# Linear-attention block on one Trainium2 core: trailing steps behind the third sum's copy, half of the last norm on VectorE, kv times wo in float32r parts

## The chip, the core and the metric

The kernel runs on one core of one Trainium2 chip. The core has a matrix engine (TensorE, PE), three engines for elementwise work (VectorE or DVE, ScalarE or ACT, GpSimd or POOL) and a queue engine (SyncE, SP) that here only starts DMA transfers; ACT and POOL start some too. Each engine works through its own instructions strictly in the order in which the program issued them, and waits at the head of that order until what it needs is there. The metric is the device time in microseconds (us) from start to end of one execution.

## The reference, cut to what matters

```python
def _A_ref(x, wqkv, wo):            # linear attention, 32 heads of 16
    qkv = (x @ wqkv).reshape(B, S, 3, H, Dh).transpose(2, 0, 3, 1, 4)
    q, k, v = qkv
    phi = lambda t: where(t > 0, t + 1, exp(t)) + 1e-6
    pq, pk = phi(q), phi(k)
    kv = einsum("bhsd,bhse->bhde", pk, v)
    z = einsum("bhsd->bhd", pk)
    num = einsum("bhqd,bhde->bhqe", pq, kv)
    den = einsum("bhqd,bhd->bhq", pq, z)[..., None] + 1e-6
    return (num / den).transpose(0, 2, 1, 3).reshape(B, S, D) @ wo

def _B_ref(x, w1, b1, w2):          # Dense -> Mish -> Dense
    h = x @ w1 + b1
    return (h * tanh(softplus(h))) @ w2

mod = (silu(c) @ w_mod).reshape(c.shape[0], 6, 1, -1)
sa, ca, ga, sb, cb, gb = six rows of mod
h = layernorm(x) * (1 + ca) + sa
x = x + ga * _A_ref(h, wqkv, wo)
h = layernorm(x) * (1 + cb) + sb
x = x + gb * _B_ref(h, w1, b1, w2)
```

The shapes are S = 2048 rows, D = 512 columns, F = 1792 hidden columns, all float32.

## The kernel before

**Precision.** Nearly every matrix product is made of three float32r products. split() makes of a tile t a high part (ACT copies t into float32r) and, one step later, a low part (DVE takes t minus the high part). mm3() adds hi x hi, hi x lo and lo x hi in PSUM. Only a few products take plain float32, among them m_ps at line 849: kv times wo, one matmul for each of four column groups, shown by the profile as eight instructions.

**Rows and tiles.** The 2048 rows are four blocks b of 512; a block is four tiles t of 128 rows. The working memory is one pool of 101 slots of 128x512 float32 (SLOTS); a tile takes a slot when it is made and gives it back after its last reader. PSUM has eight banks: four "acc", three "h", one "tp"; tiles of a tag take its banks in turn.

**The order of the work.** It is written out by hand. Work on DVE, ACT and POOL that follows a product is put into generators. spawn() adds one to a list and tick() moves every one in the list on by a step, the earliest spawned first. So the order on each engine is the order of the ticks, and within a tick the order of spawning. later(p, f, wait) waits `wait` steps and then issues the Mish of p on ACT; mish() issues Mish and high part in one step and the low part in the next.

**Attention.** wo_scale (line 474) multiplies the four tiles of wo by a row of the modulation, one tile a step, while PE builds gacc and q. z_side and kv_side prepare the small matrices that give den and kv. kv_ps (lines 830 to 840) is multiplied by a mask into kv; m_ps (847 to 850) is kv times wo, and its split parts ms are used by every o_unit. attend(b) (line 682) makes the reciprocal of den (lines 691 and 692), stores it in DRAM, loads it back spread over partitions as rd, scales q with it (706) and splits it into qs. o_unit(b, t) multiplies qs by ms; o_post adds the result to the rows r.

**The second norm.** Blocks 0 and 1 are normed before the pair stage. The eight tiles of blocks 2 and 3 are normed within it by norm_tile (line 764): first two ACT passes with sums (act_sums, lines 213 and 214), a step later a small DVE operation (218) and POOL's power (192), a step later DVE's shift nb (222) and the apply on ACT (201), a step later a POOL DMA of the tile to DRAM (775). They are read back at the start of the last pair (load_back).

**The pair stage.** The hidden layer works on pairs of row blocks and pairs of hidden tiles: a pair g makes four results c11, c12, c21, c22 of seven products (product, line 924), each two chunks of three matmuls. pair_begin makes a11 x b11 into bank pa, copies it (L940, u1), and adds a12 x b21 (c11). pair_early makes s1 x t1 into bank pc and adds s2 x t2 onto pa, copied as u2 (L958; L999 for the second of two pairs). pair_middle adds s3 x t3 onto pa, copied as u3 (L965), and c22 = pc + u3 (DVE, L935). pair_end adds a22 x t4 onto pa, whose Mish is taken straight from the bank (L899), and s4 x b22 onto pc, for c12. Since products add onto pa after a copy has read it, each copy must be done before PE writes the next.

pair_unit takes two functions as `between`: one ahead of pair_middle and one behind it. In the stage for blocks 0 and 1 (main stage) they are trail(): a norm tile is spawned, d_unit(0, f) multiplies an earlier activation by w2 (12 matmuls), and a tick follows. two_pairs interleaves pairs 0 and 1; its between[0] is a plain tick. In the stage for blocks 2 and 3 they are gap(): an e_unit and a tick. w2_job scales and splits a tile of w2 for each of two hidden tiles a pair, rows(g, wait) makes the left operands of pair g.

Of the kernel before, what the change touches and what calls it, by code (L numbers as in the profile page):

```python
# [13 lines left out]
P = 128  # L14
# [11 lines left out]
def block_kernel(ctx: ExitStack, tc: tile.TileContext, x, wqkv, wo, w1, b1t, w2, c, wmodt, out):  # L26
# [15 lines left out]
    def ps(tag, name, shape=(P, 512)):  # L42
        return psp.tile(list(shape), F32, tag=tag, name=name, bufs=PBUFS[tag])
# [4 lines left out]
    running, fresh = [], []  # L48

    def spawn(gen):  # L50
        fresh.append(gen)

    def tick():

        running.extend(fresh)
        fresh.clear()
        for g in list(running):
            if next(g, "end") == "end":
                running.remove(g)
# [11 lines left out]
    def split(name, t, keep, key, lo_engine=dve, hi_engine=act, plus=None):  # L71

        hi, lo = sb(f"{name}h", F32R, t.shape), sb(f"{name}l", F32R, t.shape)
        if hi_engine is act:
            act.activation(hi, t, AF.Copy)
        else:
            hi_engine.tensor_copy(hi, t)
        if lo_engine is dve:
            yield
        if plus is None:  # L80
            lo_engine.tensor_tensor(lo, t, f32(hi), op=ALU.subtract)
        else:
            dve.scalar_tensor_tensor(lo, t, plus, f32(hi), op0=ALU.add, op1=ALU.subtract)
        keep[key] = hi, lo
# [101 lines left out]
    def ln_eps(key, b, lo=0, hi=4):  # L186
        dve.tensor_scalar(rs[key, b][:, lo:hi], mv[key, b][:, lo:hi, 1], EPS, 1.0, op0=ALU.add, op1=ALU.mult)  # L187
# [11 lines left out]
    def ln_apply(key, b, j, t, dst, engine):  # L199
        if engine is act:  # L200
            act.activation(dst, t, AF.Identity, bias=nb[key, b][:, j:j + 1], scale=rs[key, b][:, j:j + 1])  # L201
        else:
            engine.tensor_scalar(dst, t, mv[key, b][:, j, 0:1], rs[key, b][:, j:j + 1],
                                 op0=ALU.subtract, op1=ALU.mult)

    def act_sums(key, b, t, v):

        if (key, b) not in rs:
            for d, name in (rs, "rs"), (nb, "nb"):
                d[key, b] = cst.tile([P, 4], F32, tag=name, name=f"{name}_{key}_{b}", bufs=NB)  # L210
        scrap = sb(f"scrap_{key}_{b}_{t}")
        sums = cst.tile([P, 2], F32, tag="sums", name=f"sums_{key}_{b}_{t}", bufs=6)
        act.activation(scrap, v, AF.Identity, scale=-1.0 / D, accum_out=sums[:, 0:1])
        act.activation(scrap, v, AF.Square, bias=sums[:, 0:1], accum_out=sums[:, 1:2])
        return sums

    def sums_eps(key, b, t, sums):
        dve.tensor_scalar(rs[key, b][:, t:t + 1], sums[:, 1:2], 1.0 / D, EPS, op0=ALU.mult, op1=ALU.add)  # L218
        ln_rstd(key, b, t, t + 1)

    def sums_shift(key, b, t, sums):
        dve.tensor_tensor(nb[key, b][:, t:t + 1], sums[:, 0:1], rs[key, b][:, t:t + 1], op=ALU.mult)
# [251 lines left out]
    def wo_scale():  # L474

        for k in range(4):
            dve.tensor_tensor(wos[k], wos[k], bc["ga"], op=ALU.mult)
            yield

    zc = cst.tile([P, 4], F32, name="zc")  # L480
    zh = cst.tile([P, 32], F32, name="zh")
# [282 lines left out]
    def norm_tile(b, t):  # L764

        v = xt.pop(("r", b, t))
        sums = act_sums("n", b, t, v)
        yield
        sums_eps("n", b, t, sums)
        yield  # L770
        sums_shift("n", b, t, sums)
        ln_apply("n", b, t, v, v, act)
        yield
        d = nd[b, t] = drp.tile([P, D], F32, name=f"nd_{b}_{t}")
        pool.dma_start(d, v)
# [51 lines left out]
    next(early_rows[1])  # L827
    attending = attend(0, 5)
    next(attending)
    kv_ps = ps("acc", "kv_ps")  # L830
    for g in range(4):
        for k in range(4):
# [3 lines left out]
    for j in range(2):  # L836
        js = slice(64 * j, 64 * (j + 1))
        dve.tensor_tensor(kv.rearrange("p (g m) -> p g m", g=4)[js, :, js],
                          kv_ps.rearrange("p (g m) -> p g m", g=4)[js, :, js],
                          bmask[js, js].unsqueeze(1).to_broadcast([64, 4, 64]), op=ALU.mult)  # L840
    next(attending)
    spawn(attending)
    for g in range(1, 4):
# [2 lines left out]
        tick()  # L846
    for g in range(4):
        m_ps = ps("acc", f"m_ps_{g}")
        pe.matmul(m_ps, kv[:, P * g:P * (g + 1)], wos[g], start=True, stop=True)
        spawn(split(f"m_{g}", m_ps, ms, g))  # L850
    run(early_rows[1])
    for g in range(4):
# [92 lines left out]
    def later(p, f, wait=0):  # L945
        for _ in range(wait):
            yield
        mish_b(p, f)
        yield
# [12 lines left out]
    def pair_middle(g, pa, pc, u2):  # L962
        u3, c22 = sb(f"u3_{g}"), sb(f"c22_{g}")
        product(g, "s3", "t3", onto=pa)
        act.activation(u3, pa, AF.Copy)  # L965
        add(c22, pc, u3)
        spawn(later(c22, 2 * g + 1))

    def pair_end(c0, g, pa, pc, u2):
        c12 = sb(f"c12_{g}")  # L970
        m = mish(product(g, "a22", "t4", onto=pa), c0, 2 * g + 1)
        next(m)
        spawn(m)
        product(g, "s4", "b22", onto=pc)
        add(c12, pc, u2)
        spawn(later(c12, 2 * g, 1))
        tick()

    def pair_unit(c0, g, odd, between):
        begun = pair_begin(c0, g, ("tp" if odd else "h", "h"))  # L980
        tick()
        state = pair_early(c0, g, *begun, "h")
        tick()
        between[0]()
        pair_middle(g, *state)
        between[1]()
        pair_end(c0, g, *state)

    def two_pairs(c0, g0, g1, begun, between):

        s0 = pair_early(c0, g0, *begun[0], "h")
        tick()
        pc = product(g1, "s1", "t1", "h")
        pair_middle(g0, *s0)
        tick()
        pa, c11 = begun[1]
        u2 = sb(f"u2_{g1}")
        product(g1, "s2", "t2", onto=pa)
        act.activation(u2, pa, AF.Copy)  # L999
        spawn(mish(c11, c0, 2 * g1))  # L1000
        tick()
        pair_end(c0, g0, *s0)
        between[0]()
        pair_middle(g1, pa, pc, u2)
        between[1]()
        pair_end(c0, g1, pa, pc, u2)

    def prep_a(b, f):
# [4 lines left out]
    def second(b, side):  # L1013

        for n, f in enumerate(last_first):
            side(n)
            ahead(b, n + NF)
            tick()
            d_unit(b, f, n)
# [34 lines left out]
    def norm_next():  # L1054
        if tiles:
            spawn(tiles.pop(0))

    def trail(f, side=None):
        def unit():
            norm_next()  # L1060
            d_unit(0, f, f)
            ahead(1, f)
            if side is not None:
                spawn(side)
            tick()
        return unit

    for g in range(1, G):
        for f in (2 * g, 2 * g + 1):
            spawn(w2_job(f))  # L1070
        if g == 1:
            spawn(rows(2, 3))
            norm_next()
            two_pairs(0, 0, 1, begun, (tick, trail(0, rows(3, 2))))
            store_rows(0)
        else:
            norm_next()
            pair_unit(0, g, g % 2, (trail(2 * g - 3), trail(2 * g - 2, rows(g + 2, 2) if g + 2 < G else None)))
        if g < KEPT:
            store_rows(g)  # L1080
        if g == G - 1:
            for n in range(8):
                load_back("n", nd, 2 + n // 4, n % 4)
    for f in (NF - 3, NF - 2, NF - 1):
        trail(f)()
    second(1, prepare)


# [28 lines left out]
    def e_unit(c, n):  # L1117
        g = pairs[n]
        seventh(("m1", "m2")[c], "acc", ag[L, 2 * g + c], [w[:, c, :] for w in wb[g]], n, G - 1)
# [66 lines left out]
    for n, g in enumerate(pairs):  # L1186
        if n < 5:
            if n:
                load_rows(n)
            if n:  # L1190
                load_wb(pairs[n + 1])
        if n == 5:
            load_wb(pairs[6])
            load_r(0, 0)
        if n == 6:
            for m in pairs[:5]:
                load_wt("m4", m)
        def gap(c, m):
            def unit():
                if m >= 0:  # L1200
                    e_unit(c, m)
                tick()
            return unit

        if n == 0:
            begun = [pair_begin(L, pairs[i], ("tp" if i else "h", "acc")) for i in range(2)]
            tick()
        elif n == 1:
            two_pairs(L, pairs[0], g, begun, (gap(0, 0), gap(1, 0)))
            for i in range(2):  # L1210
                spawn(left_trail(pairs[i]))
        else:
            pair_unit(L, g, n % 2, (gap(0, n - 1), gap(1, n - 1)))
            if n < EARLY:
                spawn(left_trail(g))
# [70 lines left out]
```

## Time and profile before

| what | value |
|---|---|
| median of 3 runs | 506.92 us (506.33 to 507.45) |
| the profiled execution | 505.36 us, span 503.6 us |
| mean granted TensorE clock | 0.997 |
| PE busy, matmuls | 492.7 us (98%), 2648 |
| DVE busy | 343.8 us (68%) |
| ACT busy | 294.4 us (58%) |
| POOL busy | 144.8 us (29%) |
| DMA | 98.58 MB, mean 196 GB/s |

The span is the time from the first to the last instruction; the execution's own time has some 1.8 us around it. Busy time of PE is not PE at its peak, since matmuls are pipelined and a record lasts longer than the distance to the next. A wait is written as the idle time before an instruction and what ended it. The shares are averages over stages of very different kind, so stretches of the span have to be read by themselves.

### The profile page before, as it was taken

The numbers are of one execution on the slowest core, as the hardware profiler recorded it, in microseconds if no ns is written. First come the engines' busy times: TensorE is split into PE (matmuls) and PEld (weight loads), VectorE is DVE, ScalarE is ACT, GpSimd is POOL, SyncE is SP. The second block draws the span as 40 slices with busy tenths as digits, with TensorE's granted clock in tenths as the row PEclk, the third lists the DMA queues.
The fourth block names the chain that finished last, engine by engine and source line by source line (L and its number), as shares of the span: only waits on it lengthen the run. The fifth ranks groups of instructions, "written<-read, shape, count | busy, mean of one in ns | idle before, by whom it ended". The sixth has DMA issues, their size and how long they took to land.

```text
span 503.6 us, 7666 instructions
## 1 busy us (share of the span) xinstructions
PE 492.7 (98%) x2648; PEld 414.0 (82%) x2648; DVE 343.8 (68%) x666; ACT 294.4 (58%) x532; POOL 144.8 (29%) x246
## 2 busy tenths in 40 slices
PE   7999999999999999998999999999999999999997
PEld 6788888878778888886778888888788888899997
DVE  6885664878987678966557562679953755559772
ACT  6868684724462978567988555368354555568100
POOL 3473120000213323123144210524355131445200
PEclk9999999999999999998999999999999999999999
DMA  8824753482554317439989935999999353698512
GB/s 289 297 68 88 194 128 87 129 270 72 140 136 131 84 42 235 147 117 376 303 282 336 361 123 192 285 373 337 366 366 283 90 158 83 147 230 229 127 43 85
DMA packets 66765, 98.58 MB, mean 196 GB/s; under 512 B 7405, under 2 KB 31861, under 8 KB 66726
## 3 DMA queue, kind: packets, MB, share of 16 engines
q0 software_dynamic: 29360, 45.31, 32.6%
q1 hardware_dynamic: 37220, 52.51, 32.0%
q8 instruction: 21, 0.34, 0.3%
q10 hardware_dynamic: 146, 0.26, 0.1%
q14 instruction: 18, 0.15, 0.1%
HBM read 62.92 MB, written 33.03 MB: 191 GB/s over the span
## 4 chain that ended last, share of the span: by engine, by line
PE 87%; ACT 6%; DVE 2%; issue 2%; DMA 1%; SPq 0%; DVEq 0%; ACTq 0%
PE p_a L930 16%; PE p_s L930 6%; PE m L69 5%; PE m L68 5%; PE m L67 5%; PE oacc L69 4%; PE oacc L68 4%; PE oacc L67 4%; PE o L67 3%; PE pq L67 3%; PE gacc L68 3%; PE gacc L69 3%; PE o L69 3%; PE gacc L67 3%; PE pq L69 3%; PE pq L68 3%
## 5 line engine op out<-in xcount | busy, mean ns | idle before, releaser
L935 DVE TENSOR_TENSOR c<-p_s,u 128x512 f32<-128x512 f32 x28 | 19.4, 692 | 47.1 <-PE p_s L930 25.4
L922 ACT ACTIVATE ub<-c,b1c 128x512 f32<-128x512 f32 x28 | 20.1, 718 | 7.5 <-DVE c L935 7.5
L958 ACT ACTIVATE u<-p_a 128x512 f32<-128x512 f32 x12 | 7.1, 593 | 29.4 <-PE p_a L930 29.4
L192 POOL TENSOR_TENSOR rs_n<-rs_n,half 128x1 f32<-128x1 f32 x16 | 11.1, 698 | 39.4 <-DVE rs_n L218 29.0
L1184 POOL DMA_DIRECT2D wt_m<-w2t x20 | 14.0, 704 | 26.1 <-PE m L69 17.2
L248 DVE SCALAR_TENSOR_TENSOR ku<-e_k,relu_k 128x512 f32<-128x512 f32 x16 | 11.0, 690 | 14.5 <-ACT relu_k L246 14.5
L788 ACT ACTIVATE hf_n<-tp_n,mc 128x512 f32<-128x512 f32 x16 | 11.7, 769 | 13.4 <-PE tp_n L786 13.4
L245 ACT ACTIVATE e_q<-pq 128x512 f32<-128x512 f32 x16 | 9.4, 588 | 16.3 <-PE pq L69 16.3
L940 ACT ACTIVATE u<-p_a 128x512 f32<-128x512 f32 x14 | 8.3, 596 | 17.8 <-PE p_a L930 17.8
L245 ACT ACTIVATE e_k<-pk 128x512 f32<-128x512 f32 x16 | 9.6, 598 | 13.3 <-PE pk L69 13.2
L586 POOL DMA_DIRECT2D w2b<-w2d x20 | 10.6, 549 | 18.1 <-DMA out_dram<-r 5.5
L899 ACT ACTIVATE u<-p_a,b1c 128x512 f32<-128x512 f32 x14 | 9.6, 683 | 9.9 <-PE p_a L930 9.9
L694 POOL DMA_DIRECT2D rden_d<-rden x3 | 2.2, 718 | 43.5 <-DVE rden L692 43.5
L935 DVE TENSOR_TENSOR c<-p_a,u 128x512 f32<-128x512 f32 x14 | 9.6, 690 | 7.2 <-PE p_a L930 2.4
L580 POOL DMA_DIRECT2D wb<-w2d x14 | 9.9, 712 | 14.8 <-PE m L69 8.2
L248 DVE SCALAR_TENSOR_TENSOR q<-e_q,relu_q 128x512 f32<-128x512 f32 x16 | 11.0, 688 | 4.5 <-ACT relu_q L246 4.3
L706 DVE SCALAR_TENSOR_TENSOR q<-q,rd 128x512 f32<-128x512 f32 x16 | 10.6, 688 | 4.7 <-DMA rd<-rden_d 4.7
L192 POOL TENSOR_TENSOR rs_x<-rs_x,half 128x1 f32<-128x1 f32 (+1 forms) x10 | 7.4, 744 | 22.2 <-DVE rs_x L187 21.4
L201 ACT ACTIVATE x<-x,nb_x,rs_x 128x512 f32<-128x512 f32 x15 | 11.5, 810 | 3.8 <-DVE nb_x L196 3.1
L718 DVE TENSOR_TENSOR r<-o,r 128x512 f32<-128x512 f32 x16 | 10.9, 679 | 2.3 <-PE o L69 2.3
L257 POOL DMA_DIRECT2D ku<-ku x8 | 7.2, 895 | 17.6 <-DVE ku L248 16.9
L965 ACT ACTIVATE u<-p_a 128x512 f32<-128x512 f32 x14 | 8.3, 591 | 6.2 <-PE p_a L930 6.2
(1427 smaller groups left out, 1944.1 us busy)
## 6 DMA issues: line engine op xcount, KB each, us to landing
wm<-in_wmodt_dram SPq DMA_DIRECT2D x24, 256.0 KB, 5.4
w2b<-w2d POOLq DMA_DIRECT2D x20, 256.0 KB, 6.6
wt_m<-w2t POOLq DMA_DIRECT2D x20, 256.0 KB, 3.4
r<-in_x_dram SPq DMA_DIRECT2D x16, 256.0 KB, 3.0
x<-in_x_dram SPq DMA_DIRECT2D x15, 256.0 KB, 4.8
w1p<-in_w_dram SPq DMA_DIRECT2D x14, 256.0 KB, 4.2
w2r<-in_w_dram SPq DMA_DIRECT2D x14, 256.0 KB, 3.2
wb<-w2d POOLq DMA_DIRECT2D x14, 256.0 KB, 4.3
```

The lines of the kernel that those rows point to most:

```text
L67: pe.matmul(o, st[0], mv[0], start=start, stop=False)
L68: pe.matmul(o, st[0], mv[1], start=False, stop=False)
L69: pe.matmul(o, st[1], mv[0], start=False, stop=stop)
L192: pool.tensor_tensor(y, y, half[:, lo:hi], op=ALU.pow)
L201: act.activation(dst, t, AF.Identity, bias=nb[key, b][:, j:j + 1], scale=rs[key, b][:, j:j + 1])
L245: act.activation(e, p, AF.Exp)
L248: dve.scalar_tensor_tensor(dst, e, 1.0, r, op0=ALU.min, op1=ALU.add)
L788: act.activation(hf[b, j], p, AF.Identity, bias=mc[:, 12 + j:13 + j], scale=mc[:, 16 + j:17 + j])
L922: act.activation(u, p, AF.Mish, bias=b1c[:, f:f + 1])
L930: pe.matmul(p, st, mv, start=onto is None and c == 0 and i == 0, stop=c == 1 and i == 2, skip_group_check=onto is not None)
L935: dve.tensor_tensor(out, p, u, op=ALU.add)
L1184: pool.dma_start(v, w2t[g][:, :, SUM[name], :])
```

## The change

There are three parts.

- **Ticks within a pair.** trail() and gap() no longer tick. pair_unit and two_pairs tick themselves: once behind pair_middle and once behind between[1]. So the trailing steps that came after the first d_unit or e_unit, ahead of the third sum, are now issued behind its copy u3 and c22. later(c22) gets one more step of waiting. In two_pairs between[0] of the main stage stays a tick ahead of pair_middle.
- **The last norm.** trail() spawns a norm tile only where it is given a `side`, so a pair takes two tiles in place of three. Tiles with odd t take DVE's statistics (bn_stats, bn_aggr), POOL's power in the same step, and DVE's apply a step later; tiles with even t stay as they were.
- **kv times wo.** wo_scale also splits each scaled tile, kv is split after its mask, and m_ps takes mm3 on the parts.

```diff
     def spawn(gen):
-        fresh.append(gen)
+        fresh.append(iter(gen))
...
         for k in range(4):
             dve.tensor_tensor(wos[k], wos[k], bc["ga"], op=ALU.mult)
             yield
+            yield from split(f"wos_{k}", wos[k], wos, k)
...
         v = xt.pop(("r", b, t))
-        sums = act_sums("n", b, t, v)
-        yield
-        sums_eps("n", b, t, sums)
-        yield
-        sums_shift("n", b, t, sums)
-        ln_apply("n", b, t, v, v, act)
+        if t % 2:
+            ln_stats("n", b, t, v)
+            ln_eps("n", b, t, t + 1)
+            ln_rstd("n", b, t, t + 1)
+            yield
+            ln_apply("n", b, t, v, v, dve)
+        else:
+            sums = act_sums("n", b, t, v)
+            yield
+            sums_eps("n", b, t, sums)
+            yield
+            sums_shift("n", b, t, sums)
+            ln_apply("n", b, t, v, v, act)
         yield
...
+    kvs = {}
     kv_ps = ps("acc", "kv_ps")
...
+    spawn(split("kv", kv, kvs, 0))
     next(attending)
...
-        pe.matmul(m_ps, kv[:, P * g:P * (g + 1)], wos[g], start=True, stop=True)
+        mm3(m_ps, [h[:, P * g:P * (g + 1)] for h in kvs[0]], wos[g], True, True)
...
         add(c22, pc, u3)
-        spawn(later(c22, 2 * g + 1))
+        spawn(later(c22, 2 * g + 1, 1))
...
         between[0]()
         pair_middle(g, *state)
+        tick()
         between[1]()
+        tick()
         pair_end(c0, g, *state)
...
         between[0]()
         pair_middle(g1, pa, pc, u2)
+        tick()
         between[1]()
+        tick()
         pair_end(c0, g1, pa, pc, u2)
...
     def trail(f, side=None):
         def unit():
-            norm_next()
+            if side is not None:
+                norm_next()
+                spawn(side)
             d_unit(0, f, f)
             ahead(1, f)
-            if side is not None:
-                spawn(side)
-            tick()
         return unit
...
-            pair_unit(0, g, g % 2, (trail(2 * g - 3), trail(2 * g - 2, rows(g + 2, 2) if g + 2 < G else None)))
+            pair_unit(0, g, g % 2, (trail(2 * g - 3), trail(2 * g - 2, rows(g + 2, 2) if g + 2 < G else ())))
...
     for f in (NF - 3, NF - 2, NF - 1):
         trail(f)()
+        tick()
...
         def gap(c, m):
             def unit():
-                if m >= 0:
-                    e_unit(c, m)
-                tick()
+                e_unit(c, m)
             return unit
```

## The prediction

> **What bounds the kernel now.** The page puts TensorE (PE) at 492.7 us busy of a 503.6 us span, so I looked for where PE does not run at its own pace. The first view was the busy time by stretch, cut at the starts of the column-pair products; its columns are the length, busy us (count) of PE, weight loads, VectorE (DVE), ScalarE (ACT) and GpSimd (POOL), then granted clock, DMA share and GB/s.
> ```profile
> 214.36:234.82 20.46, 18.36 (x74) 14.49 (x73) 11.58 (x23) 15.53 (x30) 5.75 (x10) 0.92 0.65 222
> 234.82:250.90 16.08, 15.29 (x67) 12.31 (x66) 9.58 (x22) 12.66 (x26) 3.24 (x5) 1.00 0.95 327
> 250.90:267.59 16.69, 15.42 (x68) 12.47 (x67) 9.83 (x23) 14.95 (x33) 6.85 (x12) 1.00 0.93 305
> 282.55:297.51 14.96, 14.96 (x68) 12.39 (x67) 9.34 (x17) 8.49 (x16) 3.20 (x6) 1.00 0.63 211
> 362.72:447.00 84.28, 84.28 (x441) 72.56 (x441) 44.36 (x71) 42.53 (x69) 33.17 (x55) 1.00 0.73 199
> ```
> A pair has seven products of 6 matmuls and two d_units of 12, 66 matmuls. Pair 5 does them in 14.96 us, 0.227 each, without a gap: that is PE's own pace. Pair 2 takes 16.08 (1.12 lost) and pair 3 16.69 (1.73 lost). The two interleaved pairs 0 and 1 have 72 matmuls from 214.36, 16.33 us at that pace, and take 20.46: 4.13 lost. The later pair stage (362.72 on) loses nothing, so reordering can only cost there. The most that the moved steps can bring is 6.98 us. The order of PE's instructions over time names the waits (start, duration, engine, line, in brackets the idle time and its releaser):
> ```profile
> 230.36 0.50 PE L930 MATMUL p_a<-t_0h,a_1h 128*128 128x512 f32 x1 [2.10 <-ACT u L965]
> 230.70 0.40 PE L930 MATMUL p_a<-t_0l,a_1h 128*128 128x512 f32 x1
> 231.18 0.63 PE L930 MATMUL p_a<-t_1h,a_1h 128*128 128x512 f32 x1
> 231.61 0.63 PE L930 MATMUL p_a<-t_1l,a_1h 128*128 128x512 f32 x1
> 234.59 0.39 PE L930 MATMUL p_s<-b_3h,s_1l 128*128 128x512 f32 x1
> ...
> 248.05 0.50 PE L930 MATMUL p_a<-t_0h,a_2h 128*128 128x512 f32 x1 [0.80 <-ACT u L965]
> ...
> 264.57 0.50 PE L930 MATMUL p_a<-t_0h,a_3h 128*128 128x512 f32 x1 [1.27 <-ACT u L965]
> ```
> All three wait for L965, the copy u3 of the third sum. The first has a second price: from 231.18 to 234.59 matmuls start 0.43 apart instead of 0.23 (231.18 to 231.61; granted clock 0.92 over the stretch), about 1.8 of the 4.13.
>
> **Why u3 is late, and what the moved steps do.** ACT's order in the two pairs, and DVE's row that holds it up:
> ```profile
> 221.86 0.73 ACT L922 ACTIVATE ub<-c,b1c 128x512 f32<-128x512 f32 x1 [0.76 <-DVE c L935]
> 223.80 0.82 ACT L201 ACTIVATE r<-r,nb_n,rs_n 128x512 f32<-128x512 f32 x1 [0.72 <-DVE nb_n L222]
> 224.52 0.71 ACT L899 ACTIVATE u<-c,b1c 128x512 f32<-128x512 f32 x1
> ...
> 229.12 0.70 ACT L922 ACTIVATE ub<-c,b1c 128x512 f32<-128x512 f32 x1
> 229.73 0.57 ACT L965 ACTIVATE u<-p_a 128x512 f32<-128x512 f32 x1
> 223.61 0.15 DVE L222 TENSOR_TENSOR nb_n<-sums_n,rs_n 128x1 f32<-128x1 f32 x1
> ```
> From 223.80 ACT runs back to back to u3 of pair 1 at 229.73.
>
> *Two pairs: slower by 0.62.* In this unit the step ahead of the third sum of pair 1 (between[0], here a plain tick) stays where it was; only the later gap moves. What changes is later(c22) of pair 0: with one more yield its Mish (ub, 221.86) no longer fills the time in which ACT waits for nb, but comes behind the apply of 223.80 (norm_tile was spawned earlier and steps first). The apply still starts at 223.80, since DVE's order up to nb is unchanged, so 0.62 (229.12 to 229.73) is inserted into the full chain: u3 near 230.35, PE's a22 near 230.98 instead of 230.36. From below the bound is 0 (the step finds a hole), from above 0.62 plus a longer slow-clock stretch, at most another 1.8. I take +0.62: the chain has no hole. The stall of 2.1 becomes 2.7 and the slow clock stays.
>
> *Pairs 2 and 3: faster by 2.85.* Here the tick with the trailing steps goes behind u3 and c22, and the three norm tiles of a pair become two, one on each engine. An ACT tile costs two passes and an apply, and an odd tile's price on DVE is in the rows of norm_each and of a scaled copy:
> ```profile
> 239.96 0.62 ACT L213 ACTIVATE scrap_n<-r 128x512 f32<-128x512 f32 x1
> 240.70 0.72 ACT L214 ACTIVATE scrap_n<-r,sums_n 128x512 f32<-128x512 f32 x1
> 241.42 0.58 ACT L958 ACTIVATE u<-p_a 128x512 f32<-128x512 f32 x1
> ...
> 182.47 0.70 DVE L183 BATCH_NORM_STATS2 st_n<-r 128x6 f32<-128x512 f32 x1
> 183.21 0.18 DVE L184 BATCH_NORM_AGGREGATE mv_n<-st_n 128x2 f32<-128x6 f32 x1
> L500 DVE TENSOR_SCALAR zs<-zbc_sb,mc 128x512 f32<-128x512 f32 x4 | 1.7, 480 | 0.0
> ```
> Passes 1.46 (239.96 to 241.42) and apply 0.72 (223.80 to 224.52): 2.18 a tile on ACT, 6.5 a pair before, 2.2 after; ACT falls from 14.95 in pair 3 to near 10.6 of 14.96. DVE gains 0.70 + 0.18 + 0.15 + 0.48 = 1.5 a pair (apply between 0.48 and the 0.69 of a two-input pass) on about 9.6. The added pow of an odd tile is queued on POOL behind the even tile's store, and DVE's apply waits for it one tick later; its result is wanted only by a store. Neither engine is full. Pair 4 shows when u3 can run once ACT is free, and DVE's trailing steps:
> ```profile
> 275.43 1.28 DVE L526 TENSOR_TENSOR w2r<-w2r,gb_bc 128x512 f32<-128x512 f32 x2
> 276.64 0.68 DVE L81 TENSOR_TENSOR a_8l<-u,a_8h 128x512 fp32r<-128x512 f32 x1
> 277.78 0.69 DVE L935 TENSOR_TENSOR c<-p_s,u 128x512 f32<-128x512 f32 x1 [0.46 <-ACT u L965]
> 278.39 0.68 DVE L81 TENSOR_TENSOR s_5l<-s,s_5h 128x512 fp32r<-128x512 f32 x1
> 277.15 0.60 ACT L965 ACTIVATE u<-p_a 128x512 f32<-128x512 f32 x1 [0.34 <-PE p_a L930]
> ```
> The pair starts at 267.59, so u3 is at +9.56 and c22 at +10.19. PE wants u3 at +12.24 (54 matmuls): 2.1 us of slack. I take the whole loss of both pairs away; the bounds are 0 and 2.85.
>
> *What is late next: +0.5.* Everything behind c22 on DVE now starts at +10.8: two low parts (0.60 each, 277.78 to 278.39), two w2 scalings (1.21, 275.43 to 276.64), and only then the even tile's nb, at +13.2. ACT's apply waits for it (+13.4), and behind it stand two w2 high parts (1.04), ub (0.62) and the Mish of the fourth sum, which reads the pair's first bank until +16.5. With three "h" banks that bank of an even pair serves the second product of the next pair, due at 14.96 + 1.36 = +16.32. That is 0.15, plus 0.1 for the slow first matmul after a wait (230.36 to 230.70), 0.25 at each of the changes 2 to 3 and 4 to 5. Bounds: 0, and 1.2 if nb comes half a us later. Odd pairs use "tp" and pairs 5 and 6 have no tile left.
>
> **kv times wo: +0.3.** The first row below is the chain of work in order of time; the rest are single instructions.
> ```profile
> 132.82 3.43 PE m_ps L849 x8
> 105.70 0.68 DVE L477 TENSOR_TENSOR wo<-wo,ga_bc 128x512 f32<-128x512 f32 x1
> 106.90 0.68 DVE L477 TENSOR_TENSOR wo<-wo,ga_bc 128x512 f32<-128x512 f32 x1
> 119.83 0.69 DVE L248 SCALAR_TENSOR_TENSOR q<-e_q,relu_q 128x512 f32<-128x512 f32 x1 [0.80 <-ACT relu_q L246]
> 123.07 0.69 DVE L81 TENSOR_TENSOR a_0l<-w1p,a_0h 128x512 fp32r<-128x512 f32 x1 [1.08 <-ACT a_0h L75]
> 139.28 0.69 DVE L706 SCALAR_TENSOR_TENSOR q<-q,rd 128x512 f32<-128x512 f32 x1 [1.29 <-DMA rd<-rden_d]
> 198.37 0.68 DVE L81 TENSOR_TENSOR qs_2l<-q,qs_2h 128x512 fp32r<-128x512 f32 x1
> 199.38 0.40 PE L69 MATMUL o<-m_2h,qs_2l 128*128 128x512 f32 x1
> ```
> PE: 3.43 becomes 12 x 0.227 = 2.72, 0.71 less. But the parts of wos put four copies on ACT (it idles there) and four subtractions on DVE, and spread wo_scale over eight steps: three scalings and four subtractions now stand between 105.70 and the q of 119.83 where two scalings stood, 5 x 0.60 = 3.0 more. Idle time takes up 1.35 (0.80 in the row, the rest in small gaps), so that q comes 1.65 later, about when the first den product wants it. The wait of 1.08 at 123.07 takes up more; some 0.55 reaches kv and the reciprocal of den. The low part of kv (0.60) hides in the wait of 1.29 at 139.28. The 0.55 itself passes through that DMA wait, for the rows of rd start from the reciprocal, and on through DVE and ACT, which run nearly full, to qs_2l of the last block. That ends at 199.05 and PE reads it at 199.38: 0.3 to spare. With PE 0.71 earlier and the chain 0.55 later PE waits 0.9 there and is 0.25 to 0.3 later than before. Bounds: -0.71 if the chain is absorbed, +1.3 if it is a us later still.
>
> **Sum.** -2.85 + 0.62 + 0.5 + 0.3 = -1.43. The profiled execution has 505.36 us for its span of 503.6, and the median of the other three is 1.56 above; that difference is kept: 506.92 - 1.43 = 505.5.
>
> **The clock.** The trace's slow stretch lasted 3.41 us (231.18 to 234.59) after a wait of 2.10, while 0.80 and 1.27 left the clock alone. [...]
>
> **Rivals.** (1) The two pairs' stall goes too: 4.13 + 0.62 less, 500.8. For it speaks that the wait is the same L965; against it that between[0] still ticks ahead of that copy. 0.04. [...] 0.12. (3) The change does not do what it says: in pairs 2 to 4 the even tile's apply, now behind DVE's whole trailing queue, holds ACT for a us a pair and the bank wait takes the place of the u3 wait: about 1.4 back, 506.9. For it: the 0.15 margin above is on the wrong side already; against it: ACT has over 4 us free. 0.25. (4) Slower: the attention chain. Ten more tiles take slots of the 101 while loads already queue for them; if rd lands 4 us later, PE's wait at 199.38 grows by 3.4: 508.9. Each us is passed on one to one, and from some 3 us (1.4 gained, 1 of threshold) it decides. Against it: the 1.29 wait is one DMA's, and most loads there are early. 0.15. My forecast has 0.44.
>
> **How the numbers follow.** A difference of 0.2%, 1.0 us, is about what a measurement of this kernel tells from no change. Faster (below 505.9): three quarters of the forecast, 0.34, with rivals 1 and 2: 0.50. Same: the rest of the forecast and most of rival 3: 0.32. Slower: rival 4 and the tail of 3: 0.18. The forecast's own range is 504.5 to 506.4. The range given, 503.4 to 507.9, goes down to rival 2 and takes in rival 3; it leaves out rival 1 and the far part of rival 4.
>
> **What would show it.** Pairs 2 to 4 at 14.96 to 15.3 us with no wait for L965; if they keep 16 or more, the main term is wrong. In the two pairs, ub of pair 0 right behind the apply, and a wait for L965 of about 2.7 us: if it is gone, rival 1. A wait for ACT's Mish of p_a (L899) at the second product of pairs 3 and 5. A wait for qs_2l some 78 us after the start of den of block 0: none if the chain was absorbed, over 3 us in rival 4. The later pair stage still without a gap.

## The result and the profile after

The changed kernel takes 502.68 us (median of six runs, 500.95 to 504.09) against 506.21 us of the kernel before (six runs, 505.2 to 507.45): a ratio of 0.993 with an interval of 0.9906 to 0.9955. The prediction was 505.5, with a range from 503.4 to 507.9. The direction was right, the size was not: the time lies below the range.

Measured a second time, beside other kernels (the last run below), the change is worth 2.6 us: 502.64 against 505.23. The profiled executions say the same: 502.79 after, 505.36 before, 2.57 less. The median of 506.92 that the prediction started from came from three runs; in the three later comparisons the kernel before had medians of 505.21 (17 runs), 505.2 (15) and 505.23 (11).

The first view answers to the prediction's first: busy time by stretch, cut at the starts of the column-pair products (length, PE, weight loads, DVE, ACT, POOL, granted clock, DMA share, GB/s). The rows are the two interleaved pairs, pairs 2 to 4, and the later pair stage.
```profile
213.84:234.72 20.88, 18.17 (x73) 14.36 (x72) 13.26 (x27) 14.22 (x26) 6.11 (x11) 0.93 0.55 182
234.72:249.90 15.18, 15.18 (x68) 12.53 (x66) 8.54 (x18) 8.35 (x17) 1.64 (x4) 0.99 0.98 337
249.90:264.86 14.96, 14.96 (x68) 12.39 (x66) 10.69 (x24) 10.51 (x21) 5.45 (x11) 1.00 1.07 371
264.86:279.82 14.96, 14.96 (x68) 12.39 (x66) 10.61 (x24) 10.51 (x21) 5.45 (x11) 1.00 0.96 325
362.00:446.00 84.00, 84.00 (x446) 72.59 (x445) 43.23 (x69) 43.16 (x71) 32.65 (x54) 1.00 0.73 196
```
Pair 3 fell from 16.53 us to 14.96, PE's own pace, and ACT's work in it from 14.79 to 10.51. (Before, PE's first product of pair 4 stands at 267.43. The prediction had used 267.59, the cut that came from the chain, and so 16.69 for the pair and 14.95 for ACT's work.) Pair 2 fell from 16.08 to 15.18; the 0.22 above PE's pace is the tail of the slow clock (the row at 234.72 below lasts 0.58). The two interleaved pairs grew from 20.46 to 20.88. The later stage still runs without a gap. The cut at 213.84 already lies 0.52 earlier than its counterpart at 214.36, so the attention gained 0.52. The whole profile difference is these four numbers: -0.52 + 0.42 - 0.90 - 1.57 = -2.57.

PE's order in time around the pairs (start, duration, engine, line; in brackets the idle time and what ended it):
```profile
230.44 0.50 PE L940 MATMUL p_a<-t_0h,a_1h 128*128 128x512 f32 x1 [2.71 <-ACT u L975]
234.72 0.58 PE L940 MATMUL p_a<-b_0h,a_2h 128*128 128x512 f32 x1
251.26 0.39 PE L940 MATMUL p_a<-b_2h,a_3h 128*128 128x512 f32 x1
```
Of the three waits for u3 (now L975) one is left, that of pair 1, and it is 2.71 where it was 2.10. The last row lies in the second product of pair 3, where the prediction had put a wait for a bank: there is none. ACT's and DVE's orders at the same places:
```profile
223.27 0.82 ACT L201 ACTIVATE r<-r,nb_n,rs_n 128x512 f32<-128x512 f32 x1 [1.84 <-DVE nb_n L222]
223.99 0.71 ACT L932 ACTIVATE ub<-c,b1c 128x512 f32<-128x512 f32 x1
...
229.82 0.57 ACT L975 ACTIVATE u<-p_a 128x512 f32<-128x512 f32 x1
...
248.49 0.82 ACT L201 ACTIVATE r<-r,nb_n,rs_n 128x512 f32<-128x512 f32 x1 [2.41 <-DVE nb_n L222]
250.87 0.67 ACT L909 ACTIVATE u<-p_a,b1c 128x512 f32<-128x512 f32 x1
```
Pair 0's ub now stands right behind the apply (223.27, 223.99), and u3 of pair 1 follows a full chain. In pair 2 the apply waits 2.41 for nb, but ACT has the time: the Mish of the fourth sum comes at 250.87 and delays nobody.

In the attention stage:
```profile
121.42 0.68 DVE L248 SCALAR_TENSOR_TENSOR q<-e_q,relu_q 128x512 f32<-128x512 f32 x1
126.90 0.95 DVE L693 RECIPROCAL rden<-rden 128x128 f32<-128x128 f32 x1
197.57 0.68 DVE L81 TENSOR_TENSOR qs_2l<-q,qs_2h 128x512 fp32r<-128x512 f32 x1
132.87 0.39 PE L67 MATMUL m_ps<-wos_0h,kvh 128*128 128x512 f32 x1
135.36 0.39 PE L69 MATMUL m_ps<-wos_3h,kvl 128*128 128x512 f32 x1
202.96 0.39 PE L940 MATMUL p_a<-b_0h,a_0h 128*128 128x512 f32 x1
```
m_ps takes 2.72 us (132.87 to 135.36 and one more step of 0.23) where it took 3.43. The q ahead of den comes 1.59 later, the reciprocal 0.41 later. PE waits for no qs_2l (it reads it at 198.86), and the first pair product starts at 202.96, in the kernel before at 203.48.

### The profile page after: what moved, and what is told of

It reads as the page before. It is cut to its first block, busy times and chain, and to the rows that moved or that the text cites. A ratio compares the mean times of both kernels' runs of the same rounds, so it can differ in the third digit from the quotient of the medians.

```text
span 501.0 us, 7672 instructions
## 1 busy us (share of the span) xinstructions
PE 491.8 (98%) x2652; PEld 414.9 (83%) x2652; DVE 349.7 (70%) x679; ACT 289.8 (58%) x517; POOL 143.2 (29%) x246
## 4 chain that ended last, share of the span: by engine, by line
PE 93%; ACT 4%; DVE 2%; DMA 1%; issue 0%; ACTq 0%
PE p_a L940 18%; PE p_s L940 7%; PE oacc L69 5%; PE oacc L68 5%; PE oacc L67 5%; PE m L69 5%; PE m L68 5%; PE m L67 5%; PE pq L67 3%; PE o L67 3%; PE gacc L68 3%; PE gacc L69 3%; PE o L69 3%; PE gacc L67 3%; PE pq L68 3%; PE o L68 3%
## 5 line engine op out<-in xcount | busy, mean ns | idle before, releaser
L192 POOL TENSOR_TENSOR rs_n<-rs_n,half 128x1 f32<-128x1 f32 x16 | 9.6, 604 | 30.7 <-DVE rs_n L218 15.0
L975 ACT ACTIVATE u<-p_a 128x512 f32<-128x512 f32 x14 | 8.3, 594 | 13.0 <-PE p_a L940 13.0
L587 POOL DMA_DIRECT2D w2b<-w2d x20 | 10.6, 550 | 18.1 <-DMA out_dram<-r 5.7
L707 DVE SCALAR_TENSOR_TENSOR q<-q,rd 128x512 f32<-128x512 f32 x16 | 10.6, 688 | 3.2 <-DMA rd<-rden_d 3.2
L783 POOL DMA_DIRECT2D nd<-r x8 | 4.6, 571 | 27.7 <-ACT r L201 26.2
```

The costliest lines, as they stand in the source:

```text
L192: pool.tensor_tensor(y, y, half[:, lo:hi], op=ALU.pow)
```

## The experiments

The theory after the result: what freed pairs 2 and 3 is ACT's lighter load, that is, the norm part, and the rival is that the moved ticks did it. In the two pairs the extra step of later(c22) costs 0.6 us of wait, and the slow clock comes on top; the rival is that it falls into a hole. The kv part gains what PE saves, because the chain through rd has more slack than the one profile of before showed; the rival is the prediction's chain that passes each delay on one to one.

**The kv part alone**, on the kernel before:
```diff
             dve.tensor_tensor(wos[k], wos[k], bc["ga"], op=ALU.mult)
             yield
+            yield from split(f"wos_{k}", wos[k], wos, k)
...
+    kvs = {}
...
+    spawn(split("kv", kv, kvs, 0))
...
-        pe.matmul(m_ps, kv[:, P * g:P * (g + 1)], wos[g], start=True, stop=True)
+        mm3(m_ps, [h[:, P * g:P * (g + 1)] for h in kvs[0]], wos[g], True, True)
```


> The kernel before with the kv times wo part alone. Theory of the prediction (a later reciprocal of den comes out one to one at the last block's qs parts): the first pair product starts 0.25 to 0.3 us later than the 203.48 of before, PE waits 0.9 us for qs_2l. Rival (the rows of rd land when the DMA queues let them, not a fixed time after the reciprocal): no wait for qs_2l, the first pair product 0.52 us earlier, near 202.96: 0.71 from m_ps less 0.19 at the first den product. Total 0.5 us less than before by the rival, 0.3 more by the prediction.

Measured: 504.63 us (504.34 to 505.35, 12 runs) against 505.21, ratio 0.9985 (0.9977 to 0.9994): 0.6 less. Its profiled execution was the slowest of the twelve, and PE's order there shows the very wait that the prediction had described:
```profile
199.45 0.50 PE L69 MATMUL o<-m_2h,qs_2l 128*128 128x512 f32 x1 [0.57 <-DVE qs_2l L81]
203.66 0.39 PE L933 MATMUL p_a<-b_0h,a_0h 128*128 128x512 f32 x1
```
There the first pair product is 0.18 later than in the kernel before, and that execution takes 505.35. So the predicted case exists, but the median says that it is not the usual one.

**A delay put into that chain**: four DVE additions whose result nobody reads, ahead of the reciprocal of the first den.
```diff
+        if b == 0:
+            idle = sb("idle")
+            for _ in range(4):
+                dve.tensor_tensor(idle, bc["ga"], bc["ga"], op=ALU.add)
```


> The kernel before with four additions of 128x512 on DVE (2.4 us, results unused) ahead of the reciprocal of den of block 0. Theory of the prediction (delay passed on one to one through the loads of rd to qs_2l): qs_2l starts 2.4 us later than 198.37, PE waits there for 2.1 us, the first pair product moves from 203.48 to 205.6, total up to 2.1 more. Rival (the loads land when the queues let them, later waits for other loads take the delay up): qs_2l within 1 us of 198.37, PE's wait below 0.7, total within 0.7 of before.

Measured: 505.57 us (11 runs) against 505.2, ratio 1.0009 (1.0 to 1.0018). DVE's order in time, with the delay and then in the kernel before:
```profile
126.05 2.87 DVE L693 TENSOR_TENSOR idle<-ga_bc 128x512 f32<-128x512 f32 x4
129.32 0.95 DVE L696 RECIPROCAL rden<-rden 128x128 f32<-128x128 f32 x1
147.61 0.95 DVE L696 RECIPROCAL rden<-rden 128x128 f32<-128x128 f32 x1
...
181.62 0.95 DVE L696 RECIPROCAL rden<-rden 128x128 f32<-128x128 f32 x1
190.99 0.69 DVE L710 SCALAR_TENSOR_TENSOR q<-q,rd 128x512 f32<-128x512 f32 x1 [1.16 <-DMA rd<-rden_d]
```
```profile
126.49 0.95 DVE L692 RECIPROCAL rden<-rden 128x128 f32<-128x128 f32 x1
146.31 0.95 DVE L692 RECIPROCAL rden<-rden 128x128 f32<-128x128 f32 x1
...
180.94 0.95 DVE L692 RECIPROCAL rden<-rden 128x128 f32<-128x128 f32 x1
191.14 0.69 DVE L706 SCALAR_TENSOR_TENSOR q<-q,rd 128x512 f32<-128x512 f32 x1 [2.03 <-DMA rd<-rden_d]
```
The delay is 2.83 us at the first block's reciprocal, 1.30 at the second's, 0.68 at the fourth's; at the last load of rd it is gone (-0.15), and PE has no wait for qs_2l. Each us is not passed on one to one. By this one execution a quarter reaches the fourth reciprocal, which stands at 180.94 in the kernel before, 181.12 with the ticks alone and 181.10 with both halves of the norm part; the last link, the landing of rd, varies by 1.6 us where the program is the same up to there, more than that quarter.

**The norm part alone**, the old ticks kept: norm_tile as in the change, and two tiles a pair.
```diff
         def unit():
-            norm_next()
+            if side is not None:
+                norm_next()
             d_unit(0, f, f)
...
```


> The kernel before with the change of the last norm alone; the ticks stay where they were. If ACT's load carries the gain: u3 of pairs 2 and 3 is issued at about +10 us of the pair against +12.24 wanted, so both pairs run at 15.0 us, the wait in the two pairs stays at 2.1, total 2.7 less than before, and the moved ticks were not needed. If the place of the ticks carries it: waits for u3 of 0.8 and more stay in pairs 2 and 3, total within 1 us of before.

Then each half of it by itself. First two tiles a pair, all on ACT (the diff just shown, norm_tile as before):

> The kernel before with one half of the norm part: two norm tiles a pair in place of three, all of them on ACT; ticks and kv times wo as before. ACT then carries 4.4 us of norm in a pair of 15 instead of 6.5. If the number of tiles carries the gain of pairs 2 and 3: both at 15.0 us, total 2.5 less than before, as with the whole norm part. If the engine carries it: waits for u3 of 0.5 and more stay in pairs 2, 3 or 4.

And three tiles a pair, the odd ones on DVE (norm_tile as in the change, norm_next() in every trail):

> The other half of the norm part: tiles with odd t on DVE, but three tiles a pair as before; ticks and kv times wo as before. ACT carries 3.3 us of norm a pair on the mean. If the engine carries the gain: pairs 2 and 3 at 15.0 us, total 2.5 less than before. If the number of tiles carries it (the tile begun ahead of the first d_unit has its passes ahead of u3): waits for u3 stay where that tile is an ACT tile.

Measured: both halves 502.7 us (501.78 to 503.32, 6 runs) against 505.21, ratio 0.9942 (0.9927 to 0.9957); two tiles on ACT 502.67 (502.24 to 503.1, 6), 0.9946 (0.9934 to 0.9959); odd tiles on DVE 502.41 (502.12 to 503.3, 6), 0.9943 (0.993 to 0.9956), these two against 505.23. PE's order with both halves:
```profile
230.39 0.50 PE L937 MATMUL p_a<-t_0h,a_1h 128*128 128x512 f32 x1 [2.09 <-ACT u L972]
234.78 0.44 PE L937 MATMUL p_a<-b_0h,a_2h 128*128 128x512 f32 x1
249.82 0.39 PE L937 MATMUL p_a<-b_0h,a_3h 128*128 128x512 f32 x1
264.78 0.39 PE L937 MATMUL p_a<-b_0h,a_4h 128*128 128x512 f32 x1
```
Pairs 2 and 3 take 15.04 and 14.96 us without a wait, while the ticks stand where they stood. PE's order with two tiles on ACT:
```profile
230.46 0.50 PE L930 MATMUL p_a<-t_0h,a_1h 128*128 128x512 f32 x1 [2.10 <-ACT u L965]
249.92 0.39 PE L930 MATMUL p_a<-b_0h,a_3h 128*128 128x512 f32 x1
264.88 0.39 PE L930 MATMUL p_a<-b_0h,a_4h 128*128 128x512 f32 x1
```
In both halves the wait of pair 1 is the only one left for u3 (2.10 in each). Pair 3 takes 14.96 us in both; pair 2 takes 15.25 with two tiles, with the tail of the slow clock at its start (0.43 from its first matmul to the second), and 15.01 with the odd tiles on DVE. Either half is enough, and the two together bring no more than one. The first half takes no work off ACT as a whole: the eight tiles now reach into pair 4 too, where ACT had been busy for 11.11 us of 14.96. One tile fewer in pair 3 leaves ACT an estimated 12.6 us of work in 14.96 (14.79 less the 2.18 of a tile), and some 2.4 us free there already let u3 come in time.

**The ticks alone**, three tiles a pair on ACT as before: trail() and gap() without a tick, a tick behind pair_middle and behind between[1], later(c22) a step longer.
```diff
+        tick()
         between[1]()
+        tick()
...
             norm_next()
+            if side is not None:
+                spawn(side)
             d_unit(0, f, f)
             ahead(1, f)
-            if side is not None:
-                spawn(side)
-            tick()
```


> The kernel before with the moved ticks alone; three norm tiles a pair, all on ACT. If the place of the ticks carries the gain of pairs 2 and 3: no wait for u3 in pairs 2 and 3, both at 15.0 us, and a wait of 2.7 in the two pairs; total 2.2 less than before. If ACT's load carries it: ACT keeps 6.5 us of norm in a pair of 15, late copies or late Mish readings stop PE in pairs 2 and 3 for 1 us or more in sum, and the total is within 1 us of before.

Measured: 510.74 us (510.4 to 511.95, 5 runs) against 505.21, ratio 1.0106 (1.0089 to 1.0123): 5.5 us slower. PE's order:
```profile
230.94 0.78 PE L930 MATMUL p_a<-t_0h,a_1h 128*128 128x512 f32 x1 [2.70 <-ACT u L965]
235.37 0.39 PE L930 MATMUL p_a<-b_0h,a_2h 128*128 128x512 f32 x1
250.33 0.39 PE L930 MATMUL p_a<-b_0h,a_3h 128*128 128x512 f32 x1
251.69 0.39 PE L930 MATMUL p_a<-b_2h,a_3h 128*128 128x512 f32 x1
254.94 0.50 PE L930 MATMUL p_s<-t_0h,s_3h 128*128 128x512 f32 x1 [1.73 <-ACT u L899]
267.91 0.39 PE L930 MATMUL p_a<-b_0h,a_4h 128*128 128x512 f32 x1
274.84 0.50 PE L930 MATMUL p_a<-t_0h,s_4h 128*128 128x512 f32 x1 [2.69 <-ACT u L940]
287.46 0.39 PE L930 MATMUL p_a<-b_0h,a_5h 128*128 128x512 f32 x1
```
Pair 2 is free of its wait (235.37 to 250.33, 14.96), so the moved ticks do what they say. But what they push back comes due in the next pairs: pair 3 takes 17.58 us and pair 4 19.55 instead of 14.96. In pair 4 the clock drops a second time: behind the wait of 2.69 matmuls start 0.42 apart from 275.44 to 278.82 instead of 0.23, and the granted clock is 0.89 from 272.00 to 287.62 us. DVE's and ACT's orders show by what the waits come:
```profile
263.77 0.69 DVE L935 TENSOR_TENSOR c<-p_s,u 128x512 f32<-128x512 f32 x1 [3.13 <-ACT u L965]
...
266.78 0.15 DVE L222 TENSOR_TENSOR nb_n<-sums_n,rs_n 128x1 f32<-128x1 f32 x1
```
```profile
254.22 0.67 ACT L899 ACTIVATE u<-p_a,b1c 128x512 f32<-128x512 f32 x1
...
266.97 0.82 ACT L201 ACTIVATE r<-r,nb_n,rs_n 128x512 f32<-128x512 f32 x1 [2.41 <-DVE nb_n L222]
...
272.27 0.67 ACT L899 ACTIVATE u<-p_a,b1c 128x512 f32<-128x512 f32 x1
274.21 0.57 ACT L940 ACTIVATE u<-p_a 128x512 f32<-128x512 f32 x1
```
The even tile's apply waits 2.41 us for nb, which stands on DVE 3 us behind c22 with the trailing steps between, and with three tiles to do ACT does not make that up: ub and the Mish (254.22 for pair 2, 272.27 for pair 3) come late and hold the next pair's banks and copies. This is the prediction's third rival, mechanism and place, in a kernel without the lighter norm. In the change the same wait of 2.41 stands at 248.49, and costs nothing.

**The kv and the norm part together**, the old ticks kept (both diffs above):

> The kernel before with the kv times wo part and the norm part, and all ticks where they were. If the moved ticks bring nothing once the norm is lighter and cost 0.6 through the extra step of later: wait in the two pairs 2.1, pairs 2 to 4 at 15.0 us, total 0.6 below the changed kernel, like the changed kernel with the extra step taken back. If the ticks help, the total is above the changed kernel and pairs 2 to 4 show waits.

Measured: 501.78 us (501.35 to 502.24, 5 runs) against 505.2, ratio 0.9937 (0.9924 to 0.9949). That is the change without its ticks, and its gain is not less than the change's (0.9941, below): with the intervals overlapping, the moved ticks as they are bring nothing that can be measured. Its profiled execution kept a granted clock of 1.0, and there a wait for u3 is left in pair 2:
```profile
230.03 0.50 PE L940 MATMUL p_a<-t_0h,a_1h 128*128 128x512 f32 x1 [2.10 <-ACT u L975]
232.93 0.39 PE L940 MATMUL p_a<-b_0h,a_2h 128*128 128x512 f32 x1
245.62 0.50 PE L940 MATMUL p_a<-t_0h,a_2h 128*128 128x512 f32 x1 [0.29 <-ACT u L975]
248.47 0.39 PE L940 MATMUL p_a<-b_0h,a_3h 128*128 128x512 f32 x1
```
Pair 2 takes 15.54 here. So by this one execution the ticks have 0.58 us to win in pair 2 when PE comes into it early, and lose 0.6 in the two pairs.

**The change, with later(c22) of pair 0 at its old length**:
```diff
-    def pair_middle(g, pa, pc, u2):
+    def pair_middle(g, pa, pc, u2, wait=1):
...
-        spawn(later(c22, 2 * g + 1, 1))
+        spawn(later(c22, 2 * g + 1, wait))
...
-        pair_middle(g0, *s0)
+        pair_middle(g0, *s0, wait=0 if c0 == 0 else 1)
```


> The changed kernel with one difference: in the two interleaved pairs of the main stage later(c22) of pair 0 has no extra step, as before. The prediction puts 0.62 us of the wait in the two pairs on it: wait for u3 near 2.1 us instead of 2.71, total 0.6 us less than the changed kernel. If the extra step is not the cause, the wait stays at 2.7.

Measured: 500.43 us (500.19 to 502.19, 5 runs) against 505.21, ratio 0.9898 (0.9881 to 0.9915). The wait for u3 is 2.10 again, 0.61 shorter, as the prediction had priced that step. The median lies 2.2 us below the change's, more than that, though on another chip (the kernel before has 505.21 beside the one and 505.23 beside the other). Four of the five executions had a clock of 0.999 or 1.0 and took 500.19 to 500.52; the fifth, with 0.996, took 502.19. Of the change's twelve executions three had such a clock (500.95, 501.18, 501.43); nine had 0.993 to 0.997 and took 502.46 to 504.25. Held against executions of the same kind, the step is worth 0.8 us where the clock stayed up (medians 500.37 and 501.18) and 0.6 where it dropped (502.19 in one execution, and a median of 502.79), about the 0.61 of the wait. The rest of the 2.2 is that the clock dropped in one of five executions here and in nine of twelve there. That the shorter wait is the cause of this is not shown: with the same wait of 2.10 the version with the kv and norm parts dropped in four of five.

**The change without between[0] of the two pairs**, the tick that is still ahead of their third sums:
```diff
-            two_pairs(0, 0, 1, begun, (tick, trail(0, rows(3, 2))))
+            two_pairs(0, 0, 1, begun, (lambda: None, trail(0, rows(3, 2))))
```


> The changed kernel without the plain tick ahead of the third sum of pair 1 in the two interleaved pairs (between[0] does nothing; its steps come with the next tick, behind u3). What stands between the apply and u3 on ACT then loses two row parts and one Mish, 1.65 us. Theory (a full ACT chain sets u3 there, and the stall of 2.7 also costs the slow clock): the wait falls to about 1.1 us, no slow stretch in the profile, total 1.6 less for the wait and up to 1.8 for the clock below the changed kernel, 499.4 to 501 on the same chip. Rival (something other than ACT's chain holds u3): wait stays above 2 us, total as the changed kernel.

**And also without the norm tile that is begun ahead of the two pairs** (it is done later, as one more of the pairs' tiles):
```diff
-            norm_next()
-            two_pairs(0, 0, 1, begun, (tick, trail(0, rows(3, 2))))
+            two_pairs(0, 0, 1, begun, (lambda: None, trail(0, rows(3, 2))))
```


> As the one before, and no norm tile is begun ahead of the two interleaved pairs, so that their ACT chain loses two passes and the apply that waits for nb; the eight tiles end a pair later. Theory: u3 of pair 1 is ready in time, no wait of PE in the two pairs, 16.4 us for them, every execution without a slow stretch, total 4.4 below the changed kernel's profile, near 498.4. If the tiles moved later stop PE elsewhere, pairs 2 to 6 show it as waits and the total is above the run before this one.

Measured: without the tick 499.37 us (499.06 to 500.95, 4 runs) against 505.2, ratio 0.9886 (0.9871 to 0.9901); without the tile too 498.15 (497.85 to 498.79, 4), ratio 0.9866 (0.9852 to 0.9879), the fastest version here. PE's waits in the first, and the two pairs by stretch in the second:
```profile
PE p_a L940 <- ACT u L975: 1.1, 1, 1.1
PE o L69 <- DVE qs_2l L81: 0.7, 1, 0.7
```
```profile
213.77:230.09 16.32, 16.32 (x74) 13.52 (x73) 10.95 (x20) 11.67 (x22) 3.37 (x7) 1.00 0.57 200
```
The two pairs then run at PE's own pace: 16.32 us where the prediction worked out 16.33. With a wait of 1.1, as the profiled execution shows it, the clock was 1.0 in all four executions of the first. The first rival's gain is real, but it takes these two edits more.

**The change once more**, beside other kernels on one chip:

> The changed kernel beside the kernel before on this chip, to hold it against the others. By its profile (span 501.0 against 503.6) the gain is 2.6 us; the median of the first six runs gives 3.5. If the first runs of before stood high, the ratio comes nearer to 0.995; if the profile missed part of the gain, it stays at 0.993.

Measured: 502.64 us (501.18 to 504.25, 6 runs) against 505.23 (11 runs), ratio 0.9941 (0.9921 to 0.9962).

## Why the prediction was right and wrong

The forecast lay 2.8 us above the time. 1.7 of that is the base, 1.1 the sum.

- **"That difference is kept: 506.92."** This step failed first. Later medians of the kernel before are 505.2, just below its profiled execution (505.36). The three runs shown stood 1.7 us too high, and a range of 506.33 to 507.45 from three runs did not tell so. Why they stood high is open.
- **Pairs 2 and 3, -2.85.** Right in mechanism: pair 3 at 14.96, pair 2 at 15.18, no wait for u3, ACT's work 10.51 where 10.6 was forecast. Measured -2.47: pair 3 had lost 1.57 and not 1.73 (the cut of 267.59), and pair 2 keeps 0.22. The prediction did not say which of the two parts, the ticks or the lighter norm, does it. The runs do: either half of the norm part is enough, and the ticks, without it, free pair 2 and lose 5.5 us as a whole.
- **Two pairs, +0.62.** Right. The wait is 2.71 (2.7 forecast), ub stands right behind the apply, the slow clock stays, and the step taken back gives 0.61 of wait. In the profiled executions the stretch grew by 0.42. The slow stretch was priced a little too high, at about 1.8: its eight matmuls (231.18 to 234.59) take 3.41 us where 1.82 is PE's own pace, 1.59 more. What was missing is that the clock does not drop in every execution, so that this price is paid in a part of them only (nine of the change's twelve).
- **"What is late next", +0.5.** Wrong, it is 0. The times were close: the Mish of pair 2's fourth sum was forecast to end 16.5 us into the pair, and ends at 251.54, +16.8. But PE's second product of pair 3 runs at 251.26, before that Mish ends, and without a wait, so it has another bank. The run with the ticks alone leaves no doubt: there the second product stands at 251.69 and the Mish begins only at 254.22. The failed step is "With three 'h' banks that bank of an even pair serves the second product of the next pair". Where ACT is full, the bank wait does come: at the third product, 1.73 us, in the run with the ticks alone. So the banks of a tag were not taken in turn here, though the description of the kernel says that they are; what order they follow was not tried.
- **kv times wo, +0.3.** Wrong, it is -0.52 in the profile, and -0.6 alone. The terms held at the front: m_ps 0.71 less; q 1.59 later (1.65 forecast); the reciprocal 0.41 later (0.55 forecast). The failed step is "The 0.55 itself passes through that DMA wait", with "0.3 to spare". The slack of 0.3 was a property of one execution, in which the last rd landed late (191.14): in the five whose program is the same up to there qs_2l ends 0.33, 1.26, 1.77, 1.79 and 2.05 us ahead of PE's reading. The fourth rival rested on the same step, "Each us is passed on one to one", and was not borne out; the latest landing in these runs cost PE a wait of 0.7.
- **The rivals.** The first did not come, and two more edits bring it. The second, a clock that stays up (1.8 less, 503.7), came in three of the twelve executions, which take 1.6 us less (medians 501.18 and 502.79); what keeps it up in these no run shows. The third did not come in this kernel, since ACT has room, as the text against it said.

The sum's own difference: +0.38 (pairs), -0.20 (two pairs), -0.5 (bank), -0.82 (kv) = -1.14.

## What to carry to other kernels

When a copy comes late on an engine that is full, lighten that engine there before reordering it: one norm tile fewer a pair, or the odd ones on DVE, gave the whole gain in pairs 2 and 3, while reordering the full engine moved the wait one and two pairs on and made it larger (0.80 and 1.27 before, 1.73 and 2.69 behind it). When steps are moved behind a point, look for the one place where the old order filled a hole (here 0.6 us, one argument), since it can eat the gain of the rest. And a slack of some tenths behind a DMA in one profiled execution is no bound on the path; neither are three runs a base for forecasting a change of half a per cent.

## What was not expected of the hardware

**Landing times of a load.** The second q<-q,rd of the last block waits for the last load of rd. In the five executions whose program is the same up to there (the kernel before, both halves of the norm part, each half, the ticks alone) it starts at 189.53 to 191.14 us, a spread of 1.6; in the seven with the kv part at 189.92 to 192.31, a spread of 2.4. The latest of them is in the version without the tick, where PE waits 0.7 us for qs_2l:
```profile
192.31 0.69 DVE L707 SCALAR_TENSOR_TENSOR q<-q,rd 128x512 f32<-128x512 f32 x1 [2.46 <-DMA rd<-rden_d]
```
That execution took 500.95 us where the other three of its kernel took 499.06 to 499.37. Where the spread comes from no run shows.

**A clock drop that comes in a part of the executions.** A slow stretch takes some 0.003 off an execution's mean granted clock: profiled executions with one have 0.996 or 0.997, the one with two has 0.992, those with none 1.0. Counted by that (0.997 or less), the clock dropped in 57 of the 94 executions of the kernels whose profiled execution has a wait of 2.1 in the two pairs: in 29 of 43 of the kernel before (beside the experiments), in one of five of the change with the old later, in four of five of the version with the kv and norm parts. With 2.71 (the change) it dropped in nine of twelve, and with 1.1 or no wait there in none of four and none of four. Waits of 0.80 and 1.27 (the kernel before) and 1.73 (the ticks alone) in other pairs were followed by no slow stretch in the traces. So the drop comes in a part of the executions at 2.10 and at 2.71, and was seen behind no wait of 1.73 or less; that it comes more often at 2.71 than at 2.10 is not shown.

By two profiled executions the drop costs some 1.6 us (1.38 + 0.22). The two pairs took 18.89 us in the profiled execution that kept the clock at a wait of 2.10 (214.04 to 232.93, the version with the kv and norm parts), so 16.79 without the wait. In the change they took 20.88 - 2.71 = 18.17, which is 1.38 more, and 0.22 are left at the start of pair 2. Why the clock drops in one execution and not in another at one and the same wait of 2.10 no run shows. What stays open too is why the drop costs the kernels with the old ticks so little: the version with the kv and norm parts took 501.35 us at a clock of 1.0 and 501.72 to 502.24 at 0.996 or 0.997. Part of it is shown, the wait of 0.29 in pair 2 that comes back when PE is early; the rest was not tried.
